# A new order of work for an attention and squared-relu kernel: first states alone, weights ahead of the second input, a sixth batch in seven products

## The chip, the cores and the metric

The kernel runs on one core of a Trainium2 chip. A core has TensorE (PE; its weight loads are shown apart as PEld), VectorE (DVE), ScalarE (ACT), GpSimd (POOL) and SyncE (SP). They work at the same time and wait for each other through semaphores; each runs its own instructions in the order in which the program gives them. Transfers between the chip's memory (HBM) and the on-chip memory (SBUF) are issued on the queues of GpSimd, ScalarE and SyncE and run on 16 shared DMA engines. TensorE writes its results to PSUM, from where the other engines take them. The metric is the device time of one execution in microseconds, as the median of several runs.

## The reference

Eight batches, each with 8 heads, 512 positions, 32 state rows and 64 channels, go through two attentions between x and state; the results become 8 * 544 = 4352 rows of 512 for a two-layer network:

```python
def _attn_ref(x, state):                       # (8,8,512,64), (8,8,32,64)
    scores = scale * np.matmul(x, state.transpose(0, 1, 3, 2))
    a = softmax over the 32 states
    xread = np.matmul(a, state)                # 512 rows per batch
    scores2 = scale * np.matmul(state, x.transpose(0, 1, 3, 2))
    a2 = softmax over the 512 positions
    sread = np.matmul(a2, x)                   # 32 rows per batch
    return np.concatenate([xread, sread], axis=2)

def _moe_ref(x, w_in, w_out, s, b):            # w_in 512x2048, w_out 2048x512
    r = np.maximum(x @ w_in, 0.0)
    g = s * (r * r) + b
    return g @ w_out
```

## The kernel before, in words

All work is cut into pieces. The list `ORDER` (lines 15 to 75) names them in one long sequence, and the last loop of the kernel (lines 724 to 727) calls them in that order. Nothing is moved afterwards: each engine gets its instructions in the order of the words. So `ORDER` alone sets what stands ahead of what on each engine and on each DMA queue. A word is a name and its arguments; a last letter A, V or G names the engine (ScalarE, VectorE, GpSimd) that does the piece.

**Loading.** `x0.g` loads the second half of batch 0's x for the heads of group g; its first half comes in as float32 by SyncE (line 215) and is cast by `castx`. `x.b` loads another batch with two transfers of 256 KB (as float16), `xn.b` the same data in another layout with four. `win.j` loads a quarter of w_in (512 of the 2048 hidden columns, two transfers of 256 KB), `wout.q` a quarter of w_out (512 KB). `st` loads the state rows of all batches but the first two, all on GpSimd's queue. The first two batches' states come on ScalarE's queue (line 216) and are cast by `casts`. `pair` and `turn` bring states into the two layouts that the matmuls want, on VectorE and through TensorE.

**Attention of batch b.** `xT` transposes x (VectorE), `T` makes the scores (TensorE), `keep` copies them out of PSUM (ScalarE), `U` transposes them, `mu` takes the maxima, `D` subtracts, `E1` is the exponential (ScalarE), `z` sums and inverts, `At` multiplies, `A` transposes back: A holds the softmax weights. For batch 0 these run in two halves of the positions (a last argument 0 or 1). `nm`, `nms`, `E2`, `a2`, `aps`, `a2T`, `V` and `srd` are the softmax over positions; all batches' `srd` feed one further small block (`lsr`, `ssr`, `P_sr`, here called the summary rows).

**Layer one.** w_in is first multiplied with a batch's states: `M.b.j` makes four hidden blocks' worth on TensorE, `Mc` casts it out of PSUM. A hidden block is then M times A: `l.b.f` (two matmuls of 512 columns, f from 0 to 15) with a relu on ScalarE; for batch 0, `lh.0.f.p` does blocks f and f+1 for half p. `s` and `sh` square the relus into the tile g on any of the three engines. `ps_h`, the PSUM pool of these blocks, has two buffers.

**Layer two**, plain: `L.b.rr.q` (line 505) adds four of sixteen hidden blocks for 128 rows; `out` evicts with scale and bias (VectorE, line 515) and stores. In seven products (Strassen's scheme in Winograd's form): g and w_out are seen as 2x2 blocks; `wsum.T1` to `T4` make differences of w_out's blocks once, `S` makes sums of g's blocks for a batch, partly in place, `P.b.u` is half of a product (8 matmuls of 256 columns; line 594 through the helper at line 137), `ev` evicts a product (line 604), `put` stores. Batches 3 to 7 and the summary rows use products; 0, 1 and 2 are plain. Both take turns in the two buffers of PSUM pool `ps_o`.

**Fillers.** `idle.n` (line 672) issues n matmuls of 512 columns on ones; nobody reads them.

The parts that the change touches are in `ORDER` and these functions:

Of the kernel before, what the change touches and what calls it, by code (L numbers as in the profile page):

```python
# [15 lines left out]
    "x0.1 x0.0 castx.1.A xT.0.1.0 casts.A idle.12 pair.0.4 castx.0.A xT.0.0.0 T.0.1.0 U.0.0 turn.0.4.A "  # L16
    "mu.0.0 D.0.V.0 E1.0.0 sb idle.12 keep.0.0 xT.0.1.1 win.0 M.1.0.0 M.0.0.1 x.1 z.0.0 xT.0.0.1 At.0.V.0 "
    "A.0.0 win.1 wout.0 T.0.0.1 U.0.1 Mc.1.0.A mu.0.1 D.0.V.1 Mc.0.0.A lh.0.2.0 xT.1.1 lh.0.0.0 keep.0.1 "
    "xT.1.0 idle.5 E1.0.1 win.2 M.0.1.0 T.1.1 sh.0.0.0.V Mc.0.1.A z.0.1 At.0.V.1 A.0.1 lh.0.6.0 lh.0.4.0 "
    "keep.1 sh.0.6.0.V sh.0.4.0.V sh.0.2.0.G L.0.1.0 lh.0.0.1 lh.0.4.1 lh.0.2.1 M.0.2.0 Mc.0.2.A lh.0.6.1 "  # L20
    "L.0.0.0 win.3 l.0.8 l.0.10 M.1.2.1 Mc.1.2.A M.0.3.0 U.1 mu.1 D.1.V l.0.11 sh.0.2.1.V wout.1 l.0.9 "
    "M.1.1.1 wout.2 Mc.0.3.V wout.3 sh.0.0.1.V M.1.3.0 E1.1 l.0.13 l.0.12 st s.0.10.2.V L.0.0.1 L.0.1.1 "
    "z.1 Mc.1.3.A x.2 s.0.12.2.A l.0.15 At.1.V s.0.8.2.G L.0.1.2 l.0.14 A.1 L.0.0.2 l.1.11 l.1.2 cps.0 "
    "s.0.14.2.A cps.1 cps.2 cps.3 Mc.1.1.V l.1.10 s.1.10.2.G l.1.6 L.0.0.3 c bias",
    "l.1.0 l.1.5 pair.4.16 xT.2 sh.0.4.1.V x.3 L.0.1.3 l.1.3 turn.4.12.V out.0.0 out.0.1 l.1.1 T.2.1 U.2 "
    "M.2.3.0 Mc.2.3.A mu.2 D.2.V l.1.9 L.0.3.0 keep.2 l.1.8 l.1.7 xT.3 s.1.8.2.A L.0.2.0 M.2.1.1 "
    "sh.0.6.1.G E1.2 M.2.2.0 l.1.12 Mc.2.1.V z.2 L.0.3.1 L.0.3.2 At.2.V l.1.14 Mc.2.2.A L.0.2.1 L.0.2.2 "
    "s.1.2.2.A s.1.6.2.G l.1.4 s.1.0.2.A A.2 l.1.15 L.0.3.3 out.0.3 l.1.13 x.4 xn.3 T.3.1 M.2.0.0 "
    "s.1.4.2.G l.2.6 U.3 s.1.14.2.V l.2.14 L.1.0.0 Mc.2.0.A l.2.4 nm.3 nms.3.A s.1.12.2.V xT.4 L.1.0.1 "
    "mu.3 D.3.G l.2.13 l.2.5 E2.3.0 L.0.2.3 out.0.2",  # L30
    "l.2.0 E2.3.1 L.1.0.2 L.1.0.3 l.2.7 out.1.0 M.3.0.0 Mc.3.0.A x.5 M.3.1.1 s.2.4.4.V l.2.1 l.2.9 "
    "L.1.1.0 L.1.1.1 E1.3 l.2.3 l.2.8 L.1.1.2 L.1.1.3 M.3.2.0 M.4.0.1 a2.3 Mc.3.1.V z.3 xn.4 At.3.G A.3 "
    "l.2.12 l.2.10 out.1.1 L.1.3.0 Mc.3.2.V l.2.2 L.1.3.1 wsum.T1.2.G s.2.12.2.A l.2.15 s.2.14.2.A l.2.11 "
    "L.1.3.2 Mc.4.0.V L.1.3.3 out.1.3 l.3.6 s.2.0.4.G T.4.1 U.4 l.3.5 l.3.2 aps.3 a2T.3.V l.3.7 L.1.2.0 "
    "nm.4 L.1.2.1 L.1.2.2 L.1.2.3 nms.4.A E2.4.0 xT.5 E2.4.1 l.3.4",
    "l.3.0 M.4.2.1 M.4.1.0 Mc.4.1.A L.2.1.0 Mc.4.2.V L.2.1.1 s.3.4.2.A l.3.11 a2.4 s.3.6.2.A l.3.10 "
    "out.1.2 s.2.8.2.G M.3.3.0 T.5.1 wsum.T3.0.V wsum.T3.1.V nm.5 l.3.1 mu.4 L.2.0.0 L.2.0.1 Mc.3.3.A "
    "nms.5.A E2.5.1 D.4.V E1.4 s.2.10.2.G L.2.1.2 aps.4 l.3.12 U.5 l.3.13 wsum.T2.2.V z.4 x.6 At.4.G "
    "L.2.0.2 L.2.0.3 a2T.4.A l.3.15 l.3.3 turn.12.16.A E2.5.0 L.2.1.3 out.2.1 xT.6 l.3.9 l.3.8 V.3.4 "
    "srd.3 M.5.0.1 l.3.14 out.2.0 Mc.5.0.A L.2.2.0 s.3.0.4.A A.4 L.2.2.1 l.4.1 L.2.3.0 L.2.3.1 l.4.2 "  # L40
    "srd.4 s.3.12.4.V L.2.2.2 L.2.2.3 M.4.3.0 s.3.8.4.V M.5.2.1 nm.2 a2.5 nms.2.V E2.2.0 Mc.4.3.A l.4.3 "
    "Mc.5.2.A out.2.2 L.2.3.2 E2.2.1 L.2.3.3 mu.5 out.2.3 l.4.4",
    "l.4.0 aps.5 P.3.0 a2.2 a2T.5.A S.3.3.2.V s.4.0.2.A s.4.2.2.A xn.5 P.3.1 ev.3.X1 S.3.1.1.V P.3.2 "
    "S.3.1.0.V S.3.2.2.V l.4.7 T.6.1 nm.6 D.5.G E1.5 xn.2 z.5 At.5.G M.5.1.0 P.3.3 l.4.9 Mc.5.1.A P.3.4 "
    "l.4.14 l.4.13 P.3.5 ev.3.Y l.4.5 l.4.6 ev.3.X2 U.6 s.4.4.2.A s.4.6.2.A aps.2 a2T.2.A P.3.6 nms.6.V "
    "wsum.T4.0.V wsum.T4.1.V S.3.4.2.V P.3.7 E2.6.0 P.3.8 l.4.10 l.4.8 ev.3.W1 E2.6.1 V.5.2 srd.2 x.7 "
    "srd.5 P.3.10 s.4.8.2.V P.3.11 xn.6 mu.6 a2.6 l.4.15 l.4.11 A.5 P.3.9 ev.3.X3 S.4.3.0.G aps.6 a2T.6.A "
    "l.4.12 ev.3.W2 l.5.10 s.4.12.4.A P.3.12 P.3.13 M.6.0.0 M.5.3.1 Mc.5.3.A l.5.1 S.4.1.0.V s.4.10.2.V "
    "Mc.6.0.A nm.0 put.3.0.0 P.4.0 l.5.3 P.4.1 l.5.11 ev.3.X4 D.6.V E1.6 P.4.2 S.4.3.1.V S.4.1.1.V P.4.3 "
    "l.5.5 S.4.2.2.V S.4.4.1.G l.5.8 M.6.2.1 ev.4.X1 ev.4.Y z.6 Mc.6.2.A At.6.G M.6.1.0 l.5.2 nms.0.A "  # L50
    "xT.7 l.5.6 E2.0.1 P.4.6 E2.0.0 xn.0 P.4.4 P.4.5 ev.4.X2 A.6 l.5.9 l.5.4 T.7.1 keep.7 P.4.7",
    "l.5.0 S.4.4.0.V l.5.7 s.5.8.4.V P.4.8 P.4.9 nm.7 l.5.13 put.3.0.1 ev.4.W1 Mc.6.1.A l.5.15 P.4.10 "
    "l.5.12 put.3.1.0 ev.4.X3 put.3.1.1 P.4.12",
    "l.6.0 P.4.11 U.7 s.5.4.2.V s.5.6.2.V l.6.11 s.5.0.4.G l.6.2 a2.0 aps.0 nms.7.A mu.7 ev.4.W2 "
    "put.4.0.0 D.7.G xn.7 put.4.0.1 l.5.14 P.4.13 ev.4.X4 P.5.0 a2T.0.A S.5.3.0.V xn.1 l.6.3 V.6.0 srd.0 "
    "M.6.3.1 s.5.14.2.V l.6.8 l.6.10 s.5.12.2.V Mc.6.3.V P.5.1 s.6.2.2.V srd.6 S.5.3.1.V ev.5.X1 l.6.4 "
    "l.6.7 S.5.1.2.V P.5.2 l.6.9 P.5.3 ev.5.Y M.7.1.1 M.7.0.0 l.6.1 S.5.2.2.V Mc.7.0.V P.5.6 Mc.7.1.A "
    "E1.7 l.6.12 P.5.7 ev.5.W1 S.5.4.0.V l.6.6 P.5.4 P.5.5 l.6.14 P.5.10 z.7 S.5.4.1.V M.7.2.0 M.7.3.1 "
    "E2.7.1 l.6.13 l.6.15 ev.5.X2 s.6.6.2.A s.6.12.4.A P.5.8 P.5.9 s.6.0.2.G Mc.7.3.V ev.5.X3 l.6.5 "
    "put.4.1.0 put.4.1.1 s.6.4.2.A P.5.11 ev.5.W2 P.5.12 P.5.13 At.7.G A.7 ev.5.X4 s.6.8.2.G l.7.12 "  # L60
    "put.5.0.0 l.7.14 P.6.0 l.7.4 l.7.15 s.6.10.2.G put.5.0.1 put.5.1.0 S.6.3.2.V P.6.1 S.6.1.2.V E2.7.0 "
    "ev.6.X1 nm.1 Mc.7.2.A l.7.7 a2.7 l.7.13 S.6.2.0.V P.6.2 P.6.3 ev.6.Y l.7.2 l.7.3 aps.7 nms.1.A "
    "E2.1.0 E2.1.1 P.6.4 P.6.6 S.6.4.0.V",
    "l.7.0 l.7.6 S.6.2.1.G P.6.5 l.7.5 a2T.7.V P.6.7 a2.1 aps.1 l.7.8 l.7.10 s.7.12.4.V a2T.1.V S.6.4.1.V "
    "ev.6.W1 V.7.1 srd.1 s.7.6.2.G l.7.1 l.7.11 s.7.0.2.G ev.6.X2 s.7.2.2.G P.6.10 P.6.8 P.6.9 put.5.1.1 "
    "P.6.11 srd.7 ev.6.X3 l.7.9 lsr.3 P.6.12 lsr.1 P.6.13 lsr.2 ssr.2.2.A lsr.8 ev.6.W2 put.6.0.0 "
    "put.6.0.1 s.7.4.2.V P.7.0",
    "lsr.0 lsr.10 P.7.2 lsr.5 ssr.0.2.A s.7.10.2.V ev.6.X4 lsr.6 s.7.8.2.V S.7.3.2.V P.7.1 lsr.11 "
# [10 lines left out]
def kernel(  # L79
# [678 lines left out]
```

## Time and profile before

| | before |
|---|---|
| median of 3 runs (lowest to highest) | 219.09 us (218.51 to 219.42) |
| the profiled execution | 218.68 us |
| its span, first to last instruction | 216.8 us |
| granted TensorE clock, mean | 0.998 |
| PE / DVE / ACT / POOL busy | 207.0 / 169.4 / 154.7 / 105.0 us |
| last matmul of the chain begins | 211.78 us |
| HBM read / written | 25.72 / 8.91 MB |

Busy times are unions over a span that has two quite different stages, the opening with the loads and the rest, so shares of the whole span say little; the views by stretch and the chain of waits say more. In the slices each digit is the busy share of 5.4 us in tenths. A pair of figures such as "602 ns" for a group is the mean of one instruction; matmuls are pipelined, so sixteen in a row take much less than sixteen means, and their pace is read from the chain.

### The profile page before, as it was taken

What the parts mean: (1) busy time and instruction counts of PE and PEld (TensorE: products, weight loads), DVE (VectorE), ACT (ScalarE), POOL (GpSimd) and SP (SyncE); (2) the same over time, 40 slices, a digit from 0 to 9 for tenths busy, and PEclk for the clock granted to TensorE, in tenths of its full rate; (3) what the DMA queues carried; (4) which work ended last, traced back from release to release, by engine and by line L of the source; (5) the groups of instructions that cost most, each with busy time, mean ns of one, the idle gap of its engine ahead of it and who ended that gap; (6) DMA issues with size and microseconds to landing.
All of it is one profiled execution on the core that took longest, in us unless ns stands there. A gap on an engine that the chain in (4) does not pass through costs nothing.

```text
span 216.8 us, 4729 instructions
## 1 busy us (share of the span) xinstructions
PE 207.0 (95%) x1920; PEld 126.4 (58%) x1920; DVE 169.4 (78%) x236; ACT 154.7 (71%) x262; POOL 105.0 (48%) x102
## 2 busy tenths in 40 slices
PE   7668999999999999999999999999999999999992
PEld 2334444344444434545677666776667777888881
DVE  2699885989867879986998799979887964785571
ACT  4378987898858788899889899667668866444400
POOL 8529123494679930525254318836564334225330
PEclk9999999999999999999999999999999999999999
DMA  6999992759497262192908850718903600450055
GB/s 153 186 205 205 199 197 42 125 124 133 106 173 120 48 99 49 38 155 55 144 9 137 139 110 4 97 39 139 205 10 65 131 0 3 87 111 0 0 153 141
DMA packets 23657, 22.42 MB, mean 103 GB/s; under 512 B 4436, under 2 KB 17492, under 8 KB 23636
## 3 DMA queue, kind: packets, MB, share of 16 engines
q0 software_dynamic: 16848, 12.52, 40.8%
q1 hardware_dynamic: 5504, 8.66, 16.4%
q10 hardware_dynamic: 1284, 0.95, 1.6%
q8 instruction: 15, 0.25, 0.5%
q14 instruction: 6, 0.05, 0.1%
HBM read 25.72 MB, written 8.91 MB: 160 GB/s over the span
## 4 chain that ended last, share of the span: by engine, by line
PE 90%; ACT 5%; DMA 2%; DVE 0%; issue 0%; SPq 0%
PE hps L461 24%; PE ops L505 19%; PE opf_X L137 16%; PE opf_W L137 8%; PE mps L137 4%; PE opf_Y L137 4%; PE hps_sr L461 3%; PE vps L137 2%; DMA xf<-in_x_dram 2%; ACT M L152 2%; PE aps L137 2%; PE ops_sr_X L137 2%; PE T_None L137 2%; ACT rh L491 1%; PE dps L672 1%; PE hph L137 1%
## 5 line engine op out<-in xcount | busy, mean ns | idle before, releaser
L465 ACT ACTIVATE r<-hps 128x512 f16<-128x512 f32 x120 | 67.5, 602 | 27.8 <-PE hps L461 26.3
L461 PE MATMUL hps<-A,M 128*128 128x512 f16 x240 | 64.7, 380 | 0.0
L137 PEld LDWEIGHTS <-g 128*128 128x128 f16 x480 | 46.6, 98 | 11.4 <-issue 0.7
L505 PE MATMUL ops<-w_out,g 128*128 128x512 f16 x192 | 46.3, 379 | 0.0
L471 POOL TENSOR_TENSOR g<-r 128x1024 f16<-128x1024 f16 (+1 forms) x14 | 30.4, 2180 | 23.7 <-ACT r L465 23.7
L461 PEld LDWEIGHTS <-M 128*128 128x128 f16 x240 | 21.7, 98 | 22.7 <-issue 6.2
L505 PEld LDWEIGHTS <-g 128*128 128x128 f16 x192 | 18.7, 98 | 22.2 <-issue 0.4
L152 ACT CAST M<-mps 128x1024 f16<-128x1024 f32 x22 | 22.3, 1017 | 1.6 <-PE mps L137 1.5
L469 ACT ACTIVATE g<-r 128x1024 f16<-128x1024 f16 (+1 forms) x18 | 21.4, 1210 | 0.1
L192 POOL DMA_DIRECT2D xn<-in_x_dram x32 | 18.6, 592 | 5.6 <-PE vps L137 4.9
L346 POOL TENSOR_TENSOR At<-E,rz 128x1024 f16<-128x1024 f16 x5 | 9.8, 1964 | 22.0 <-ACT r L465 11.3
L137 PE MATMUL opf_X<-w_T,g 128*128 128x256 f16 x160 | 19.8, 272 | 0.0
L575 DVE TENSOR_TENSOR g<-g 128x1024 f16<-128x1024 f16 (+1 forms) x20 | 17.9, 908 | 1.1 <-POOL S L575 0.9
L575 POOL TENSOR_TENSOR g<-g 128x1024 f16<-128x1024 f16 x4 | 8.8, 2207 | 19.6 <-PE opf_X L137 12.4
L471 DVE TENSOR_TENSOR g<-r 128x1024 f16<-128x1024 f16 (+1 forms) x18 | 14.7, 836 | 1.6 <-ACT r L465 1.6
L152 DVE CAST M<-mps 128x1024 f16<-128x1024 f32 x10 | 12.1, 1213 | 3.5 <-PE mps L137 3.0
L604 DVE SCALAR_TENSOR_TENSOR osx<-opf_X,sb_bc,bias_bc 128x512 f32<-128x512 f32 x15 | 11.2, 746 | 4.0 <-PE opf_X L137 3.9
L292 DVE STREAM_TRANSPOSE xT<-xh 128x1024 f32<-128x1024 f32 (+2 forms) x12 | 10.4, 869 | 4.7 <-ACT xh L152 4.1
L325 POOL TENSOR_TENSOR Dm<-U,mu 128x1024 f32<-128x1024 f32 x3 | 5.7, 1913 | 15.0 <-DVE mu L321 15.0
L465 ACT ACTIVATE r_sr<-hps_sr 128x256 f16<-128x256 f32 x16 | 6.1, 382 | 7.9 <-PE hps_sr L461 7.2
L137 PE MATMUL mps<-w_in,stT 64*32 64x512 f16 x256 | 11.2, 383 | 0.3
L515 DVE SCALAR_TENSOR_TENSOR osb<-ops,sb_bc,bias_bc 128x512 f32<-128x512 f32 x12 | 8.8, 737 | 3.4 <-PE ops L505 3.4
(101 smaller groups left out, 324.3 us busy)
## 6 DMA issues: line engine op xcount, KB each, us to landing
out_dram<-osx SPq DMA_DIRECT2D x36, 128.0 KB, 2.4
xn<-in_x_dram POOLq DMA_DIRECT2D x32, 128.0 KB, 5.1
xh<-in_x_dram POOLq DMA_DIRECT2D x14, 256.0 KB, 5.1
w_in<-in_moe_w_in_dram POOLq DMA_DIRECT2D x8, 256.0 KB, 8.3
w_out<-in_moe_w_out_dram POOLq DMA_DIRECT2D x4, 512.0 KB, 11.2
out_dram<-osb SPq DMA_DIRECT2D x16, 128.0 KB, 2.6
out_dram<-osb SPq DMA_DIRECT2D x16, 64.0 KB, 4.4
xf<-in_x_dram SPq DMA_DIRECT2D x2, 256.0 KB, 3.7
```

The costliest lines, as they stand in the source:

```text
L137: return nc.tensor.matmul(out, lhsT, rhs, start=start, stop=stop, tile_position=tp, is_transpose=is_transpose, skip_group_check=skip,)
L152: (engine.copy if engine is nc.scalar else engine.tensor_copy)(out, in_)
L192: nc.gpsimd.dma_start(out=xn_t[b][32 * jh : 32 * jh + 32].rearrange("t h c d -> t h (c d)"), in_=x[b].rearrange("h (t jh c) d -> jh t h (c ...
L292: nc.vector.transpose(part(out, p, g), part(in_, p, g))
L346: e.tensor_tensor(out, E1, over_n(rz), ALU.mult)
L461: nc.tensor.matmul(hps, lhsT, rhs, start=(i == 0), stop=(i == len(terms) - 1))
L465: nc.scalar.activation(R_t[tag, q][:, i], hps, AF.Relu)
L469: nc.scalar.activation(g, r, AF.Square)
L471: e.tensor_mul(g, r, r)
L505: nc.tensor.matmul(ops_t[tag, rr], G_t[tag][:, f, P * rr : P * rr + P], w_out_f(f), start=(f == 0), stop=(f == NKF - 1),)
L575: e.tensor_tensor(out, x, y, op)
L604: nc.vector.scalar_tensor_tensor(out, fast(b, name[0]), s_bc, out if plus else bias, ALU.mult, ALU.add)
```

## The change

- ScalarE's queue loads only batch 0's states (`stf` has 2 rows of tiles instead of 4); `st` gets a range, and is called twice: `st.2.4` for batch 1 as GpSimd's third transfer, and `st.4.16` for the others. `pair` and `turn` are called three times instead of twice.
- On GpSimd's queue the three first blocks of w_in stand ahead of x.1; `wout.0` follows x.1, then win.3, wout.1, the other states, x.2, wout.2 and wout.3.
- Batch 2's layer two is in seven products: no `L.2` and `out.2`, but `S.2`, `P.2`, `ev.2` and `put.2`, and the `wsum` pieces earlier.
- Fillers: 5 matmuls (2, 2 and 1) instead of 29 (12, 12 and 5).
- The order of everything, and which engine does many of the squares, casts, sums and multiplications, is new. Among them: `castx.0` and `Mc.1.0` on VectorE, `D` of batch 0's second half and `At.1` on GpSimd, and `U.0.1` and `mu.0.1` ahead of `z.0.0`.

The diff, cut to its core (the first group of words in full, then the places of batch 2, and the end):

```diff
-    "x0.1 x0.0 castx.1.A xT.0.1.0 casts.A idle.12 pair.0.4 castx.0.A xT.0.0.0 T.0.1.0 U.0.0 turn.0.4.A "
-    "mu.0.0 D.0.V.0 E1.0.0 sb idle.12 keep.0.0 xT.0.1.1 win.0 M.1.0.0 M.0.0.1 x.1 z.0.0 xT.0.0.1 At.0.V.0 "
-    "A.0.0 win.1 wout.0 T.0.0.1 U.0.1 Mc.1.0.A mu.0.1 D.0.V.1 Mc.0.0.A lh.0.2.0 xT.1.1 lh.0.0.0 keep.0.1 "
-    "xT.1.0 idle.5 E1.0.1 win.2 M.0.1.0 T.1.1 sh.0.0.0.V Mc.0.1.A z.0.1 At.0.V.1 A.0.1 lh.0.6.0 lh.0.4.0 "
-    "keep.1 sh.0.6.0.V sh.0.4.0.V sh.0.2.0.G L.0.1.0 lh.0.0.1 lh.0.4.1 lh.0.2.1 M.0.2.0 Mc.0.2.A lh.0.6.1 "
-    "L.0.0.0 win.3 l.0.8 l.0.10 M.1.2.1 Mc.1.2.A M.0.3.0 U.1 mu.1 D.1.V l.0.11 sh.0.2.1.V wout.1 l.0.9 "
-    "M.1.1.1 wout.2 Mc.0.3.V wout.3 sh.0.0.1.V M.1.3.0 E1.1 l.0.13 l.0.12 st s.0.10.2.V L.0.0.1 L.0.1.1 "
...
+    "castx.1.A xT.0.1.0 castx.0.V xT.0.0.0 casts.A pair.0.2 x0.0 turn.0.2.A xT.0.0.1 x0.1 T.0.1.0 U.0.0 "
+    "st.2.4 keep.0.0 xT.0.1.1 win.0 T.0.0.1 keep.0.1 mu.0.0 pair.2.4 win.1 D.0.V.0 E1.0.0 U.0.1 idle.2 "
+    "idle.2 mu.0.1 win.2 z.0.0 At.0.V.0 turn.2.4.A x.1 D.0.G.1 A.0.0 M.0.0.1 sb Mc.0.0.A idle.1 wout.0 "
+    "E1.0.1 z.0.1 At.0.V.1 A.0.1 M.0.1.0 Mc.0.1.A M.1.0.1 Mc.1.0.V xT.1.0 lh.0.2.0 sh.0.2.0.G lh.0.6.0 "
+    "lh.0.0.0 lh.0.0.1 lh.0.2.1 lh.0.6.1 sh.0.6.0.G xT.1.1 M.0.2.0 win.3 Mc.0.2.A T.1.1 sh.0.0.0.V "
+    "lh.0.4.1 l.0.11 sh.0.0.1.V l.0.9 wout.1 L.0.0.0 U.1 mu.1 D.1.V keep.1 l.0.8 l.0.10 E1.1 M.0.3.0 "
+    "Mc.0.3.V z.1 M.1.1.1 lh.0.4.0 st.4.16 L.0.1.0 Mc.1.1.A l.0.13 sh.0.4.0.V x.2 l.0.14 M.1.2.0 Mc.1.2.V "
+    "pair.4.16 M.1.3.1 l.0.15 L.0.1.1 s.0.8.2.G Mc.1.3.A wout.2 wout.3 l.0.12 turn.4.12.A At.1.G A.1 "
+    "L.0.0.1 s.0.12.2.A s.0.10.2.G l.1.11 s.0.14.2.G xT.2 l.1.2 cps.0 T.2.1 U.2 mu.2 x.3",
+    "l.1.0 l.1.9 L.0.0.2 keep.2 l.1.10 l.1.8 M.2.0.1 D.2.G E1.2 cps.1 Mc.2.0.A cps.2 cps.3 c L.0.0.3 bias "
...
+    "l.2.0 L.1.3.2 s.2.0.2.V M.3.3.0 Mc.3.3.A M.4.2.1 l.2.4 L.1.3.3 l.2.2 L.1.2.0 L.1.2.1 s.2.12.4.A "
+    "L.1.2.2 M.4.1.1 A.3 M.4.0.0 l.3.10 Mc.4.1.A out.1.3 s.2.4.2.G l.3.4 Mc.4.2.V E1.4 wsum.T4.1.V "
+    "wsum.T4.0.V s.2.2.2.V L.1.2.3 out.1.2 l.3.7 P.2.0 P.2.1 l.3.9 wsum.T3.1.V l.3.2 T.5.1 Mc.4.0.A "
+    "wsum.T3.0.V S.2.3.2.V ev.2.X1 l.3.1 P.2.2 l.3.11 l.3.8 s.3.8.4.A nm.5 nms.5.V S.2.1.2.V S.2.2.2.V "
+    "P.2.3 ev.2.Y x.6 z.4 S.2.4.1.G aps.4 l.3.5 E2.5.0 l.3.15 P.2.4 P.2.5 l.3.3 ev.2.X2 P.2.6 xT.6 l.3.14 "
...
-    stf = konst.tile([P, 4, D], FP32, name="stf")
+    stf = konst.tile([P, NG, D], FP32, name="stf")
...
-    nc.scalar.dma_start(stf, rows[:, 0:4])
+    nc.scalar.dma_start(stf, rows[:, 0:NG])
...
-    def load_states():
-        nc.gpsimd.dma_start(stn[:, 4:], rows[:, 4:])
+    def load_states(i0, i1):
+        nc.gpsimd.dma_start(stn[:, i0:i1], rows[:, i0:i1])
...
-        "castx": cast_x, "casts": lambda e: copy(e, stn[:, 0:4], stf), "pair": pair_states, "turn": turn_states,
+        "castx": cast_x, "casts": lambda e: copy(e, stn[:, 0:NG], stf), "pair": pair_states, "turn": turn_states,
```

In the words of the close, before and after, the summary rows' first product and sums change places: before, `P_sr.0` stands ahead of `P.7.10` and `S_sr.2` is two halves on VectorE; after, `P_sr.0` follows `P.7.13`, and `S_sr.2`'s second half is GpSimd's.

## The prediction

> **What bounds the kernel now.** I read the page's busy table and slices first, then the windows by stage, the chain that ended last, the timelines of the opening and of the close, and the landings of the transfers.
>
> ```profile
> PE 207.0 (95%) x1920; PEld 126.4 (58%) x1920; DVE 169.4 (78%) x236; ACT 154.7 (71%) x262; POOL 105.0 (48%) x102
> ...
> PE   7668999999999999999999999999999999999992
> ...
> DMA  6999992759497262192908850718903600450055
> ```
>
> TensorE is full from the fourth slice on; the transfer engines are full in the first six slices (32 us) and half idle later. So there are two stages. Windows, with columns: stretch, its length, busy time and instructions of PE, PEld, DVE, ACT, POOL, then granted clock, DMA share, GB/s:
>
> ```profile
> 20.00:26.00 6.00, 5.55 (x61) 2.33 (x59) 5.35 (x6) 5.41 (x10) 1.58 (x3) 1.00 1.23 200
> 26.00:32.00 6.00, 6.00 (x35) 2.66 (x28) 5.16 (x7) 5.30 (x10) 1.90 (x1) 1.00 1.47 197
> 32.00:213.00 181.00, 180.65 (x1701) 114.38 (x1699) 145.44 (x199) 132.39 (x227) 89.14 (x77) 1.00 0.50 88
> ```
>
> From 26 us on TensorE never waits, so a microsecond of matmuls taken out there is a microsecond off the end, and a faster other engine is worth nothing. Before that, the chain that ended last (start, duration, what) runs over a transfer, filler matmuls and ScalarE's casts:
>
> ```profile
> 1.22 4.38 DMA xf<-in_x_dram
> 8.25 2.70 PE dps L672 x12
> 11.36 1.94 ACT M L152 x2
> ...
> 72.72 3.45 PE ops L505 x16
> ...
> 102.26 1.75 PE opf_X L137 x16
> ```
>
> Timelines of the opening and the close:
>
> ```profile
> 3.14 0.15 PEld L672 LDWEIGHTS <-ones 128*128 128x128 f16 x1 [0.28 <-issue]
> 3.57 0.15 PEld L672 LDWEIGHTS <-ones 128*128 128x128 f16 x1 [0.28 <-issue]
> 3.99 1.02 PEld L672 LDWEIGHTS <-ones 128*128 128x128 f16 x5 [0.28 <-issue]
> ...
> 12.01 0.71 DVE L361 STREAM_TRANSPOSE A<-At 128x512 f16<-128x512 f16 x1
> ...
> 18.24 0.71 DVE L361 STREAM_TRANSPOSE A<-At 128x512 f16<-128x512 f16 x1
> ...
> 212.69 0.48 DVE L706 SCALAR_TENSOR_TENSOR osr<-ops_sr_X,sb_bc,bias_bc 128x256 f32<-128x256 f32 x1 [0.39 <-PE ops_sr_X L137]
> ```
>
> The reader is to see: sixteen plain layer-two matmuls take 3.45 us, sixteen of the product kind 1.75; the first fillers' weight loads are 0.43 us apart, the last five stand within 1.02; the two halves of batch 0's A are there at 12.72 and 18.95; TensorE's last result is evicted from 212.69, and eviction and store take the 4.1 us to the end. The profiled execution took 218.68 us around its 216.8 us span, 0.41 under the 219.09 median. I sum differences and subtract them from the median.
>
> **1. Batch 2 in seven products (gain, on the path).** Gone are four row groups of 16 matmuls at 3.45 us: 13.8. Added are 14 half products of 8 matmuls at 0.875: 12.25. Difference -1.55. Off TensorE, VectorE loses four plain evictions (4 x 0.737 = 2.95) and gets seven product evictions (7 x 0.746 = 5.2) and three full sums (3 x 1.22 = 3.66): +5.9. GpSimd gets two half sums at 2.13. The cover is the idle time of VectorE, 181 - 145 = 36 us in 32 to 213. Stores stay eight of 128 KB on SyncE's queue.
>
> **2. Where that cover is thinnest.** The weight differences T3 and T4, row groups 2 and 3 of batch 1's evictions, and batch 2's sums all come between l.2.0 and P.2.4. Counting from the end of l.2.0 along VectorE's new order with the rows: out.1.3 ends at 3.95 (it waits for L.1.3.3), the M eviction (1.21), two halves of T4 (0.68 each) and a square (0.69) reach 7.2, while TensorE gets to P.2.0 at 8.45. From there out.1.2 (to 8.8), two T3 halves, S.2.3 (1.22), the first eviction (0.75), nm.5 (1.21), a scale (0.14), S.2.1 and S.2.2 (1.22 each) end at 15.9; TensorE reaches P.2.4, which needs S.2.2, after 16.0. So a margin of 0.1 here; at the plain places there is more than 1 us. GpSimd has 20 us more to do in all (words of the order times row means: 102 to 123 us), squares above all, at 1.94 or 3.6 us each. No row shows these neighbours together: from below 0 (the margins hold), from above one late sum per batch, 5 batches x 0.2 = 1.0. I take +0.2, near the lower end, since the same kind of order gave 180.65 busy of 181 us before.
>
> **3. The opening: what lands when.** GpSimd's queue holds eight transfers: the ninth issue (w_out, 6.70) waited for the first landing. It is never empty until 35.5 us. Landings before (issue plus the trace's time to landing): x of batch 0 at 7.3, w_in block 0 at 10.6, x.1 12.85, w_in 1 15.6, w_out quarter 0 17.9, w_in 2 21.2, w_in 3 23.8, w_out quarters 26.5, 29.05, 31.6, states 32.8, x.2 35.5. Bytes are the same after (64 KB less beside them on ScalarE's queue, 32 KB of states inserted), so I keep the spacings (2.55 to 2.8 us a block): w_in 0, 1, 2 at 10.5, 13.1, 15.9, x.1 18.3, w_out 0 20.9, w_in 3 23.7, w_out 1 26.4, states 27.6, x.2 30.3, w_out 2 32.9, w_out 3 35.4. GpSimd's issues stand behind work: w_out.0 behind D.0's second half (it waits for mu.0.1, 11.5, and ends at 12.5), win.3 behind two half squares (1.18 each, done near 18.2), wout.2 and 3 behind s.0.8. All are early enough: w_in 3 needs the queue only at 20.9.
>
> **4. The opening: what computes when.** The cast of x half 0 moves to VectorE (no such row; ScalarE's 0.62 and VectorE's 0.69 for a copy out of PSUM bound it; I take 0.62), and batch 0's state transpose (0.2 by half of 0.27) now stands behind it: T begins near 6.9, not 6.78. VectorE then goes U.0.0 to 8.1, a transpose of x 0.43, mu 0.69, a state transpose 0.2, D 0.69 (10.1), and now U.0.1 0.72 and mu.0.1 0.69 ahead of z.0.0 and its reciprocal 0.93, At 0.65, A 0.71: A.0.0 at 13.8 (was 12.72). The second half needs only z, At and A after that, 2.3: A.0.1 at 16.15 (was 18.95). The half layers run from 14 us, with relus of 0.6 each, to 19.4; T.1 follows x.1 to 20.2; four l of batch 0 and L.0.0.0 to 23.2; M.0.3 waits for w_in 3 until 23.8. By 23.85 the old kernel had done one half layer (0.44) and one quarter group of L (0.86) more, and two l (0.86) fewer: the new one is 0.45 behind. Then T.2 waits for x.2 and its transpose (30.3 + 1.2 = 31.5) at a point TensorE reaches at about 31.2: 0.3. Filler matmuls, 29 before and 5 after, only fill waits now; the 2.70 us ones on the old chain are paid for by M.0.0 waiting for w_in 0 to land at 10.5 in either kernel. Sum of the opening +0.7; bounds -0.5 (blocks land 0.6 sooner, no wait for x.2) and +1.8 (each late by 0.5 more).
>
> **5. The close.** The last summary layer, its sums and products keep their shapes; S_sr.2 goes half to GpSimd (1.1 us) and is done about 3.2 us after the last summary hidden block starts, P_sr.2 reached at 3.9. Cost 0, tail 4.1 as before.
>
> **Sum:** -1.55 + 0.2 + 0.7 = -0.65; 219.09 - 0.65 = 218.4.
>
> **A rule against the change.** The first seven filler matmuls are 0.43 us apart, the last five about 0.22, though the granted clock reads 1.00 throughout. So this trace shows TensorE at half pace in its first 2.7 us of work, and the new order opens with no filler: its first dense stretch is the half layers at 14 us. At half pace those take 0.87 each instead of 0.44 and, until 18 us, are hidden by the wait for w_in 3: sum unmoved. The Trainium skill, "TensorE: Matmul & The Clock Gate", Part 1, says that half rate is the default, that about 3.4 us of sustained work releases it and an idle window as long brings it back; the trace agrees on the release, and no run shown has the return. By that rule the gaps after each transfer could bring it back, and the sum would be that of the second rival.
>
> **Rivals.**
> *The opening is even or ahead.* For it: the second half of A is 2.8 us sooner and M.0.1 and M.0.2 have their weights 2.5 and 5.3 us sooner. Against: w_in 3, x.2 and w_out end where they ended. With -0.5 for the opening: -1.55 - 0.5 + 0.1 = about -2.0, 217.1.
> *TensorE stays at half pace (ends slower).* The work from 14.2 to 23.8 us is about 6.5 us at full pace. At half pace throughout it takes 13, to 27.2: +3.4, that is 221.8. The wait for w_in 3 hides it up to about 19.5; after that each us at half pace costs 0.5. The gain is gone at about 21 us, and the kernel is slower by over 1.1 us if half pace lasts past 23. For it: 24 fewer filler matmuls and gaps from 7 to 14 us. Against: the old kernel, with PE busy 1.58 of 3 us at 11 to 14, kept its pace.
> *VectorE or GpSimd becomes the bound near the sums.* With margins of 0.1 and sums on GpSimd of 2.13, a delay of 0.2 to 0.4 in each of six product batches gives back 1.2 to 2.4: 219.1 to 220.7, 219.9 in the middle. Against: VectorE's 36 us of idle.
>
> **Numbers.** About 0.5%, 1.1 us, is what a measurement of this kernel tells from no change. Forecast 0.38 (0.12 of it faster by more, 0.26 within). Opening ahead 0.30, all faster. Half pace 0.14 (0.11 slower, 0.03 within). VectorE or GpSimd 0.18 (0.11 slower, 0.07 within). Together faster 0.42, same 0.36, slower 0.22. The range runs from 216.3 (opening ahead by 1.3) to 220.8 (the upper end of the VectorE case), leaving the long half pace out. The forecast's own range is 217.4 to 219.4.
>
> **What would show it.** Step 1: 64 matmuls fewer at L505, 112 more of the product kind, none waiting. Step 2: PE 99% busy between 36 us and the end; if not, a wait on S or on a VectorE eviction near P.2.4 names the rival. Step 3: w_in 3 landing near 23.7, x.2 near 30. Step 4: A's two transposes ending near 13.8 and 16.2, M.0.3 near 23.8; and the spacing of the first half layers' weight loads tells half pace (0.22 for 256 columns) from full (0.11). I am wrong if the transfers' order moves landings by more than a microsecond, since nearly all the opening hangs on them.

## The result

| | before | after |
|---|---|---|
| median of 20 runs (lowest to highest) | 219.01 us (218.26 to 220.32) | 220.62 us (219.03 to 221.40) |
| the profiled execution | 218.68 us | 220.73 us |
| its span | 216.8 us | 219.0 us |
| the last product of the summary rows begins | 211.78 us | 213.97 us |

The ratio is 1.0071, with a 95% interval of 1.0053 to 1.0089: the changed kernel is 0.7% slower, by 1.6 us. I had forecast 0.65 us faster. The time lies inside my range; the direction was wrong.

The lines of functions stand one further down in the new kernel: layer one's matmuls are L462, layer two's plain ones L506, the product helper L138, the eviction of a product L605, the sums S L576, stores L614, w_in's loads L201. First its page, with the busy table and the slices:

```profile
PE 204.5 (93%) x1944; PEld 129.2 (59%) x1944; DVE 174.0 (79%) x238; ACT 153.1 (70%) x257; POOL 127.6 (58%) x114
...
PE   0799889999999999999899999999999999999992
...
DMA  6999999359980390006707390698663600170046
```

TensorE works 2.5 us less than before and the span is 2.2 us longer, so it waits more than it did. The saving is small for what was taken out: the fillers alone went from 8.1 to 2.5 us and the products save 1.55, so the other matmuls take some 4.7 us longer; the opening runs at half pace for longer (below). One slice in the middle (the twentieth, 104 to 110 us) shows an 8 where before there were only nines. The windows say where; columns are the stretch, its length, busy time and instructions of PE, PEld, DVE, ACT, POOL, then granted clock, DMA share and GB/s:

```profile
20.00:26.00 6.00, 4.80 (x38) 1.98 (x36) 4.49 (x4) 4.77 (x9) 4.39 (x6) 1.00 1.10 156
26.00:32.00 6.00, 6.00 (x48) 2.43 (x46) 4.89 (x8) 5.73 (x9) 5.12 (x5) 1.00 1.44 197
32.00:213.00 181.00, 179.27 (x1736) 118.11 (x1733) 149.07 (x198) 131.34 (x223) 105.27 (x84) 1.00 0.49 86
100.00:120.00 20.00, 18.89 (x202) 13.28 (x201) 18.36 (x28) 15.36 (x28) 13.42 (x13) 1.00 0.60 103
120.00:213.00 93.00, 93.00 (x991) 70.79 (x989) 73.21 (x102) 62.69 (x110) 48.62 (x36) 1.00 0.45 80
```

From 20 to 26 us TensorE is busy 4.80 us (5.55 before) and the transfers move 156 GB/s (200 before). From 100 to 120 it misses 1.11 us. From 120 on it is full. What TensorE waited for, in us in total, times, longest:

```profile
PE sps L138 <- DMA ident<-ident_const: 5.2, 1, 5.2
PE mps L138 <- DMA w_in<-in_moe_w_in_dram: 1.4, 2, 1.0
...
PE opf_W L138 <- DVE osx L605: 0.7, 1, 0.7
...
PE T_None L138 <- DVE xT L293: 0.6, 1, 0.6
PE opf_X L138 <- POOL g L576: 0.4, 1, 0.4
```

The first is the start: without the old fillers TensorE's first matmul comes at 5.25 us, where the old kernel's came at 1.46. The second and fourth belong to the opening (M.0.1 and M.0.3, and T.2), the third and fifth to the middle, and all are waits of the new order. The chain that ended last (start, duration, what) ties the opening's together:

```profile
5.07 8.12 DMA w_in<-in_moe_w_in_dram
13.23 1.05 PE mps L138 x12
14.28 0.98 PE hph L138 x4
15.28 0.61 ACT rh L492
15.97 2.03 POOL g L472 x2
18.00 1.24 POOL w_in L201 x2
19.24 0.77 POOL w_out L207
20.01 1.03 POOL stn L230
21.04 0.50 POOL xh L184
21.54 9.93 DMA xh<-in_x_dram
31.56 1.26 DVE xT L293
32.86 0.64 PE T_None L138 x16
...
213.97 0.89 PE ops_sr_X L138 x8
```

Read it from the top: w_in's second block lands at 13.19, M.0.1, the first half layers, their relu, two half squares on GpSimd, and only then the two issues of w_in's fourth block, with everything that follows on that queue, down to x.2, which T.2 waits for. The trace has w_in's fourth block issued at 17.95 and 18.62, and the quarter of w_out ahead of it had fully landed at 21.14. The transfers move 198 and 207 GB/s in the two microseconds from 17 to 19 us, then 151 to 172 from 19 to 23, 100 from 23 to 24, and 205 again from 25 to 26: the queue ran thin behind the late issue. The block landed at 23.23 and 24.64.

In the middle, VectorE's timeline has the first eviction of batch 3's products with 1.32 us of idle ahead of it:

```profile
106.09 0.75 DVE L605 SCALAR_TENSOR_TENSOR osx<-opf_X,sb_bc,bias_bc 128x512 f32<-128x512 f32 x1 [1.32 <-PE hps L462]
106.75 1.21 DVE L337 TENSOR_REDUCE z<-E 128x32 f32<-128x1024 f16 x1
108.00 0.35 DVE L338 RECIPROCAL rz<-z 128x32 f32<-128x32 f32 x1
108.27 0.65 DVE L605 SCALAR_TENSOR_TENSOR osx<-opf_Y,sb_bc,osx 128x512 f32<-128x512 f32 x1
```

The matmul that is named as its releaser (PE hps) is not one that it reads, so it was another. The evicted tile `osx0` exists once (`bufs=1`), and batch 2, now in products too, had just written it. Its four stores were issued from 98.57 to 100.44; the last of them landed at 105.91, 5.5 us after its issue and 0.18 us ahead of the eviction. The transfers issued from 97 to 108 us (KB each, median us from issue to landing):

```profile
out_dram<-osx SPq DMA_DIRECT2D x8, 128.0 KB, 4.6
xn<-in_x_dram POOLq DMA_DIRECT2D x4, 128.0 KB, 5.7
```

Over the whole run such a store takes 2.7 us; here four loads of `xn` were issued from 99.61 on, beside them. That the loads slowed the stores is likely but not shown: no run moves them away. The late eviction puts the second one (opf_Y) at 108.27, after which TensorE may take the bank again (0.7 us of wait), and puts VectorE's and GpSimd's sums late (0.4 us more).

### The profile page after: what moved, and what is told of

Its sections match the earlier page's. It is cut to its first block, busy times and chain, and to the rows that moved or that the text cites. A ratio compares the mean times of both kernels' runs of the same rounds, so it can differ in the third digit from the quotient of the medians.

```text
span 219.0 us, 4791 instructions
## 1 busy us (share of the span) xinstructions
PE 204.5 (93%) x1944; PEld 129.2 (59%) x1944; DVE 174.0 (79%) x238; ACT 153.1 (70%) x257; POOL 127.6 (58%) x114
## 4 chain that ended last, share of the span: by engine, by line
PE 81%; DMA 8%; POOL 5%; DVE 3%; issue 1%; ACT 0%; POOLq 0%; DVEq 0%
PE hps L462 22%; PE opf_X L138 19%; PE ops L506 11%; PE opf_W L138 9%; PE opf_Y L138 5%; DMA xh<-in_x_dram 5%; DMA w_in<-in_moe_w_in_dram 4%; PE mps L138 4%; PE hps_sr L462 3%; PE vps L138 2%; PE aps L138 2%; PE ops_sr_X L138 2%; POOL w_in L201 1%; PE T_None L138 1%; POOL g L576 1%; POOL g L472 1%
## 5 line engine op out<-in xcount | busy, mean ns | idle before, releaser
L462 PE MATMUL hps<-A,M 128*128 128x512 f16 x240 | 65.2, 380 | 0.2 <-ACT rh L492 0.2
L138 PEld LDWEIGHTS <-g 128*128 128x128 f16 x576 | 56.0, 98 | 15.1 <-issue 1.2
L472 POOL TENSOR_TENSOR g<-r 128x1024 f16<-128x1024 f16 (+1 forms) x10 | 27.5, 2749 | 24.2 <-ACT r L466 24.2
L462 PEld LDWEIGHTS <-M 128*128 128x128 f16 x240 | 21.6, 98 | 21.6 <-issue 6.6
L506 PE MATMUL ops<-w_out,g 128*128 128x512 f16 x128 | 31.6, 379 | 0.0
L576 POOL TENSOR_TENSOR g<-g 128x1024 f16<-128x1024 f16 x10 | 21.2, 2122 | 17.6 <-PE hps L462 10.8
L153 ACT CAST M<-mps 128x1024 f16<-128x1024 f32 x23 | 23.7, 1045 | 2.5 <-PE mps L138 2.5
L138 PE MATMUL opf_X<-w_T,g 128*128 128x256 f16 x192 | 24.1, 273 | 0.4 <-POOL g L576 0.4
L506 PEld LDWEIGHTS <-g 128*128 128x128 f16 x128 | 12.2, 98 | 14.8 <-issue 0.8
L472 DVE TENSOR_TENSOR g<-r 128x1024 f16<-128x1024 f16 (+1 forms) x19 | 17.6, 943 | 3.9 <-ACT r L466 3.9
L605 DVE SCALAR_TENSOR_TENSOR osx<-opf_X,sb_bc,bias_bc 128x512 f32<-128x512 f32 x18 | 13.4, 742 | 9.2 <-PE opf_X L138 4.3
L576 DVE TENSOR_TENSOR g<-g 128x1024 f16<-128x1024 f16 (+1 forms) x20 | 18.9, 955 | 0.3
L347 POOL TENSOR_TENSOR At<-E,rz 128x1024 f16<-128x1024 f16 x6 | 11.5, 1913 | 12.6 <-DVE rz L338 11.6
L470 ACT ACTIVATE g<-r 128x1024 f16<-128x1024 f16 (+1 forms) x13 | 18.7, 1453 | 0.1
L138 PE MATMUL mps<-w_in,stT 64*32 64x512 f16 x256 | 12.7, 404 | 1.4 <-DMA w_in<-in_moe_w_in_dram 1.4
L138 PE MATMUL opf_W<-w_T,g 128*128 128x256 f16 x96 | 12.1, 272 | 0.7 <-DVE osx L605 0.7
L326 POOL TENSOR_TENSOR Dm<-U,mu 128x1024 f32<-128x1024 f32 (+1 forms) x4 | 7.6, 1903 | 8.1 <-DVE mu L322 8.1
L138 PE MATMUL opf_Y<-w_out,g 128*128 128x256 f16 x96 | 12.3, 273 | 0.0
```

Of the source, the lines that this page charges most:

```text
L138: return nc.tensor.matmul(out, lhsT, rhs, start=start, stop=stop, tile_position=tp, is_transpose=is_transpose, skip_group_check=skip,)
L153: (engine.copy if engine is nc.scalar else engine.tensor_copy)(out, in_)
L347: e.tensor_tensor(out, E1, over_n(rz), ALU.mult)
L462: nc.tensor.matmul(hps, lhsT, rhs, start=(i == 0), stop=(i == len(terms) - 1))
L470: nc.scalar.activation(g, r, AF.Square)
L472: e.tensor_mul(g, r, r)
```

## The experiments

The ratios are against runs of the kernel before on the same chip, whose medians were 218.84 to 219.09 us. Differences between kernels are given below with each kernel's own median of before subtracted first: the changed kernel is 1.61 us above it, the kernels with the fourth block earlier, with two tiles and with both are 0.71 above, 0.45 above and 0.49 below. "Last product" is the begin of the summary rows' last product in the profiled execution, 211.78 before and 213.97 after; from 120 us on TensorE is full in both, so it says when all before it was done.

| kernel | median us | ratio (95% interval) | last product |
|---|---|---|---|
| fourth block of w_in issued earlier | 219.55 | 1.0032 (1.0015 to 1.0048) | 212.44 |
| two evicted tiles | 219.29 | 1.0016 (0.9997 to 1.0035) | 211.58 |
| both | 218.36 | 0.9977 (0.9955 to 0.9999) | 211.22 |
| both, fillers first | 218.49 | 0.9986 (0.9965 to 1.0006) | 212.08 |
| both, fillers that hold the clock | 218.72 | 0.9997 (0.9979 to 1.0016) | 211.83 |
| fillers first alone | 220.61 | 1.0079 (1.0057 to 1.0101) | 213.70 |
| two tiles, x.1 ahead of w_in 1 | 221.38 | 1.0106 (1.0085 to 1.0126) | 214.38 |
| batch 2 plain | 222.89 | 1.0174 (1.0141 to 1.0207) | 213.79 |
| batch 2 plain, w_in 3 earlier | 221.62 | 1.0129 (1.0109 to 1.0149) | 213.60 |
| old first group of words | 225.14 | 1.0281 (1.0258 to 1.0303) | 217.93 |
| old first two groups | 224.88 | 1.0268 (1.0251 to 1.0285) | 218.35 |
| old order, products put in | 231.81 | 1.0599 (1.0572 to 1.0626) | 224.21 |

### The fourth block of w_in issued ahead of the squares

```diff
-... lh.0.2.0 sh.0.2.0.G lh.0.6.0 ... M.0.2.0 win.3 Mc.0.2.A ...
+... lh.0.2.0 win.3 sh.0.2.0.G lh.0.6.0 ... M.0.2.0 Mc.0.2.A ...
```

> The changed kernel with one word moved: the issue of w_in's fourth block stands ahead of GpSimd's two half squares of batch 0. Theory (the late issue emptied the queue, so every later landing slid by about 1.2 us): the block lands by 23.8 instead of 24.64 us, w_out and x.2 a microsecond sooner too, M.0.3 begins near 23.8, the time drops by 1.0 to 219.6 us. Rival (the transfer engines were slow for another reason, or TensorE's half pace carries the opening): landings and time move by less than 0.3 us, 220.4 or more.

Measured 219.55, which is 0.90 us less than the changed kernel. The fourth block was issued at 13.06 instead of 17.95. The block itself landed at 24.50, hardly sooner than 24.64 and not by 23.8 as expected; but w_out's second quarter, x.2 and w_out's last quarter landed at 26.77, 30.49 and 35.60 (27.75, 31.47 and 36.60 in the changed kernel): all about 1 us sooner. So the late issue is one of the causes, for about a microsecond. The timed runs carry this more than the landings, since two executions with the late issue had landings as early as these; the section on TensorE's pace says why.

### Two buffers for the evicted tile of the first row half

```diff
-... tag=f"osx{key}", bufs=1)
+... tag=f"osx{key}", bufs=2 if key == "0" else 1)
```

> The changed kernel with a second buffer for the tile in which products are evicted for the first two row groups, so that batch 3's first eviction need not wait for batch 2's stores to land. Theory: VectorE's 1.3 us wait at 106.1 us goes, and with it TensorE's waits of 0.72 at 108.3 and 0.39 at 112.2; time 1.1 lower, 219.5 us. Rival (VectorE and GpSimd are simply too full there): the waits move by less than 0.2 and the time stays at 220.4 or more.

Measured 219.29, which is 1.16 us less than the changed kernel. The eviction now starts at 103.71, and TensorE has no gap in the same window:

```profile
103.71 0.74 DVE L598 SCALAR_TENSOR_TENSOR osx<-opf_X,sb_bc,bias_bc 128x512 f32<-128x512 f32 x1
```
```profile
100.00:120.00 20.00, 20.00 (x261) 14.66 (x260) 19.68 (x30) 17.14 (x30) 13.39 (x12) 1.00 0.58 94
```

The stores themselves were no quicker (5.5 us at the median); nobody waits for them. The relus of layer one run 0.97 us later in the changed kernel than here up to 104 us and 2.38 later from 117 us on, so the wait for the stores, with what followed it, cost 1.41 us in the profiled execution. It is the second buffer that shows that the eviction waited for the stores; the trace alone does not name them.

### Both together

> The changed kernel with both edits that helped alone: w_in's fourth block issued ahead of the half squares, and two buffers for the evicted first row groups. Theory (the late issue costs 0.8, the wait for stores 1.2, and they lie in different places): 220.4 - 2.0 = 218.4 us, a ratio of 0.998. Rival (the two are one delay seen twice, since the first run showed a shorter store wait too): 219.2.

Measured 218.36: 0.94 less than with two buffers alone and 1.20 less than with the earlier issue alone. So the two costs add up, and without them the change is a gain of 0.2% (0.01% to 0.45%). It has the lowest median of the study. The windows from 20 us of the changed kernel, and then of this one, show the hole in the transfers closed (last column, GB/s):

```profile
20.00:23.00 3.00, 2.82 (x16) 1.15 (x13) 2.93 (x3) 2.63 (x5) 2.13 (x4) 1.00 1.16 160
23.00:26.00 3.00, 1.98 (x24) 0.83 (x23) 1.56 (x2) 2.14 (x5) 2.25 (x2) 1.00 1.04 151
```
```profile
20.00:23.00 3.00, 2.92 (x16) 1.15 (x13) 2.93 (x3) 2.89 (x5) 0.99 (x2) 1.00 1.24 206
23.00:26.00 3.00, 2.62 (x27) 1.12 (x26) 2.19 (x3) 2.78 (x6) 2.26 (x2) 1.00 1.56 191
```

### x.1 ahead of w_in's second block

```diff
-... pair.2.4 win.1 D.0.V.0 ... turn.2.4.A x.1 D.0.G.1 ...
+... pair.2.4 x.1 win.1 D.0.V.0 ... turn.2.4.A D.0.G.1 ...
```

> The changed kernel with two buffers for the evicted row groups (219.3 us so far) and x.1 put back on the queue ahead of w_in's second block, as in the old load order. Theory (the new sequence of matmuls wants w_in's second block at 13 us, and x.1 not before 18): the block lands near 15.8, the half layers of the second block and all behind them start up to 2.5 us later, part of it absorbed by the later wait for w_in's fourth block: 220.3 to 221.3 us. Rival (batch 1's attention is what the opening waits for): 218.8 or less.

Measured 221.38, 2.08 more than the two-buffer kernel that it is made from. w_in's second block landed at 15.65 instead of 13.21, the half layers and with them GpSimd's half squares came later, and the fourth block behind those was issued only at 20.42. The queue then ran nearly dry (41 GB/s from 20 to 23 us, 152 from 23 to 26). So the new place of w_in's blocks is right for this order; a good part of the 2.08 is the same late issue, made worse, and the run does not separate the two.

### The pace of TensorE: fillers first, and fillers that hold the clock

```diff
-"castx.1.A xT.0.1.0 castx.0.V ...
+"idle.12 castx.1.A xT.0.1.0 castx.0.V ...
```

> The changed kernel with the old twelve filler matmuls put first again; nothing else. The clock records of the runs so far show full pace from 4.1 us in the old kernel but only from 11.5 to 17.2 us in the executions of the new opening. Theory (the late release of the clock is a part of the opening's loss, about 0.5 us of it, and of its spread): full pace from about 4 us, the first half layers 0.44 instead of 0.87 us, the end 0.3 to 0.8 sooner, 219.6 to 220.1 us, with less spread. Rival (the opening waits for transfers, and half pace is hidden behind them): no change, 220.4, with the weights landing where they did.

Measured 220.61: nothing gained. The windows of this run show why it says little on the price:

```profile
5.00:12.00 7.00, 4.42 (x54) 1.65 (x51) 6.64 (x15) 2.41 (x7) 4.58 (x8) 1.00 1.17 164
12.00:19.00 7.00, 6.21 (x37) 3.01 (x37) 5.10 (x9) 4.92 (x8) 2.79 (x4) 0.52 1.17 195
19.00:40.00 21.00, 19.83 (x174) 8.06 (x173) 15.99 (x19) 18.13 (x28) 17.62 (x18) 1.00 1.15 173
```

The granted clock was back at half from 11.94 to 18.76 us, in an opening with gaps. The same fillers on top of both mends:

> Both mends and the twelve fillers first. Theory (clock release worth 0.5 on its own): 217.9 us, faster than the kernel before by 0.4%. Rival (fillers hidden or in the way): as the run with both mends alone, 218.4.

Measured 218.49 beside 218.36: no gain, and again full pace only from 7.01 to 10.43 and then from 17.25. So I put fillers into the gaps as well (12 first, 8 after the first scores, 5, 5 and 5 where the new order had 2, 2 and 1, which is 6 and 4 more around the casts, and 3 more behind M.0.1):

> The kernel with both mends (win.3 ahead of the half square, two buffers for the evicted tile of row group 0) and filler matmuls placed so that TensorE has no long gap from about 4 us on (12 first, 8 after the first scores, 9 and 1 more around the casts, 3 after M.0.1). It prices the half pace of TensorE. Theory that half pace costs something: granted full pace from about 5 us on and not given back, the bias copy 0.3 to 1.0 us sooner than with the mends alone (37.24), time 217.6 to 218.0. Rival, that half pace lies wholly beside the waits for w_in: the same pace, the bias copy unmoved, 218.2 to 218.6.

Now full pace was granted from 4.31 us to the close, and the time was 218.72. The bias copy, a mark that all of these kernels have after the same work, came at 37.85 against 37.24 with both mends and no fillers. So with the issue moved up, half pace in the opening had no price that these runs could show; that the fillers themselves took time is possible, and a loss of a few tenths under them can't be excluded.

With the late issue it is another matter. Five profiles have the fourth block of w_in behind the half squares; in all of them the issue hangs on the same chain, which begins when w_in's second block lands (us from the start):

| kernel | full pace for good from | second block landed | fourth block issued | in between | x.2 landed | bias copy |
|---|---|---|---|---|---|---|
| batch 2 plain | 11.53 | 12.84 | 16.93 | 4.09 | 30.41 | 37.51 |
| two evicted tiles | 12.17 | 13.21 | 17.31 | 4.10 | 30.50 | 37.60 |
| the changed kernel | 15.82 | 13.19 | 17.95 | 4.76 | 31.47 | 38.57 |
| fillers first alone | 18.76 | 13.71 | 18.47 | 4.76 | 31.54 | 38.64 |
| two tiles, x.1 ahead of w_in 1 | 20.85 | 15.65 | 20.42 | 4.77 | 33.29 | 40.40 |

Where full pace came before the block had landed, the chain took 4.1 us; where it came later, 4.8. Its first matmuls, M.0.1, show the pace, first in the changed kernel, then with two tiles:

```profile
13.23 1.05 PE L138 MATMUL mps<-w_in,stT 64*32 64x512 f16 x15 [0.33 <-DMA w_in<-in_moe_w_in_dram]
```
```profile
13.26 0.62 PE L131 MATMUL mps<-w_in,stT 64*32 64x512 f16 x15 [0.63 <-DMA w_in<-in_moe_w_in_dram]
```

So half pace made the issue 0.7 us later, and x.2 landed 1 us later in the changed kernel than with two tiles. The first three rows have the same words up to the bias copy. With the issue moved up the bias copy follows no such order: full pace from 16.35, 17.24 and 18.39 us went with 37.24, 37.74 and 37.53 (both mends; the issue alone; the issue with batch 2 plain). No run holds full pace with the late issue in place, so how much of its price is the half pace's was not timed.

### Batch 2 plain in the new order

The words `P.2`, `S.2`, `ev.2` and `put.2` give way to `L.2` and `out.2` at the same places; T3 and T4 stay.

> The changed kernel with batch 2's layer two plain again: the 14 half products replaced in place by 16 quarter groups, sums and product evictions left away, four plain evictions put in. Theory: 13.8 instead of 12.25 us of matmuls (+1.55), but batch 3 has no stores to wait for (-1.1): +0.45, 221.1 us, with no wait of TensorE for evictions near the first products. Rival (the products cost elsewhere all that they save, even without the store wait): 219.5 or less; rival (VectorE bound later anyway): 222 or more.

Measured 222.89, against 219.29 for the two-buffer kernel, which has the same opening and no wait for stores either. The profiled executions differ by 2.21 at the last product. Timed it is 3.6; both profiled executions were the fastest of their runs, 1.7 and 0.9 us under the medians, so the profiles show less of it. I did it once more on the mended opening (`win.3` moved as in the first experiment):

> The kernel with both mends (218.36), but batch 2's layer two plain in the changed kernel's order (T3 and T4 stay where the products want them, one buffer for the evicted tile, which no store of batch 2 holds now). The products' worth with the mended opening, timed a second way after the earlier pair (222.89 against 219.29 timed, 2.1 apart in the profiles). Theory: the products bring 1.6 to 2.1, so 219.9 to 220.5, and TensorE's last matmul 1.6 to 2.2 after the one with both mends (212.1), at 213.7 to 214.3. Rival (the earlier pair's timed 3.6 is real and its profile was a lucky execution): 221.9 or more.

Measured 221.62, 3.0 more than with both mends, and 2.38 at the last product. In this order the products are worth at least the 1.55 us that I had summed. The rest is not all explained: the plain pieces stand where the products' did, not where they would be best, and the time from the last product to the end of the span was 5.6 us in both of these kernels and 5.0 to 5.1 in all others, the kernel before included. Their last store took 2.9 and 2.8 us to land, where it took 2.3 in the changed kernel and with two tiles; why is open.

### The old opening and the old order

> The old kernel's opening, word for word up to the bias, then the new order for everything that is left (batch 2 in seven products). Theory (the opening costs 2.4 us, products give 1.55, the store wait takes 1.1): 219.0 - 1.55 + 1.1 = 218.6 us, and TensorE at 99% after 40 us but for the store wait. Rival (the new order loses its time in the middle): 220 us or more.

With the old kernel's first group of words ahead of the new rest the time was 225.14. The two orders do not fit: in 34 to 37.8 us TensorE is busy 1.79 of 3.8 us, since T.2 and its transposes now come behind the bias row. This says nothing on the new opening. So I tried the seam later, after two groups:

> The first two lines of the order before (its whole opening up to the second line's end) and then the changed kernel's order, with two buffers for the evicted tile of row group 0: the products without the new opening, with a better seam than in the earlier try. Theory (the new opening costs 1.4 to 2.4 us, the products bring 1.55, the store wait cost 1.2): 218.84 - 1.55 = 217.3, and no PE wait over 0.5 us from 40 us on. Rival (the opening is not what costs, or the products bring less): 218.8 or more with TensorE full behind the seam.

Measured 224.88. TensorE is full from 80 us on (and 20.00 of 20 in 100 to 120), but from 40 to 80 it misses 5.1 us. The chain runs there over GpSimd (D, a multiplication, two differences of w_out, squares), and after the longest wait the clock falls. Windows, and then TensorE's timeline:

```profile
70.00:74.00 4.00, 1.18 (x6) 0.42 (x5) 0.75 (x1) 1.26 (x4) 3.92 (x5) 1.00 0.31 66
74.00:77.40 3.40, 3.40 (x9) 1.20 (x8) 1.97 (x5) 2.96 (x7) 0.00 (x0) 0.50 0.98 154
77.40:80.00 2.60, 2.60 (x26) 0.94 (x25) 2.60 (x5) 1.22 (x2) 0.00 (x0) 1.00 0.00 0
```
```profile
73.36 0.59 PE L455 MATMUL hps<-A,M 128*128 128x512 f16 x2 [2.82 <-ACT r L459]
73.79 1.69 PE L499 MATMUL ops<-w_out,g 128*128 128x512 f16 x4
...
78.28 1.04 PE L499 MATMUL ops<-w_out,g 128*128 128x512 f16 x4
```

Four matmuls of 512 columns take 1.69 us at half pace and 1.04 behind it, and in the trace their starts are 0.43 apart instead of 0.21.

> The order before with nothing changed but batch 2's layer two in seven products, its pieces put where the plain ones stood and T3 and T4 made earlier, and two buffers for the evicted tile of row group 0. It isolates the products. Theory: 1.55 us of matmuls less on a full TensorE, 217.3, PE busy 205.4. Rival (VectorE or GpSimd late around batch 2's sums, since nothing else was rearranged for them): 218.5 or more, with TensorE waiting for a sum S or an eviction near 95 to 112 us.

The third try left the old order as it was and put only batch 2's products in (with T4 made earlier, two evicted tiles, and the first states in the memory of one of the products' sums, as in the try before). Measured 231.81, the worst of all. TensorE is busy but for 1.2 us from 40 to 86 us and then waits for batch 2's sums, which VectorE reaches late:

```profile
PE opf_X L130 <- DVE g L568: 6.3, 1, 6.3
PE hps L454 <- ACT r L458: 4.1, 3, 2.8
```
```profile
86.35 1.24 DVE L310 STREAM_TRANSPOSE U<-T_None 128x1024 f32<-128x1024 f32 x1
87.51 1.18 DVE L538 TENSOR_TENSOR w_T<-w_out,w_T 128x2048 f16<-128x2048 f16 x1
88.61 1.21 DVE L329 TENSOR_REDUCE z<-E 128x32 f32<-128x1024 f16 x1
89.86 0.35 DVE L330 RECIPROCAL rz<-z 128x32 f32<-128x32 f32 x1
90.13 4.00 DVE L568 TENSOR_TENSOR g<-g 128x2048 f16<-128x2048 f16 x2
```

The differences of w_out, a transpose and two sums stand in one row on VectorE, and TensorE waits 6.3 us for the last; here too the clock falls to half behind the wait, from 90.42 to 97.25 us. So a clean measurement of the products under the old opening or in the old order failed three times, each on a new wait that the mixing of the orders made; it stays open. What the runs do show is that the products only pay with the rest rearranged around them.

## Why the prediction was wrong

**Step 1, the products: the matmuls right, the stores put at nothing.** 64 plain matmuls fewer, 112 of the product kind more and 24 fillers fewer make 1944 instead of 1920. The two pairs with batch 2 plain show the gain, in this order, to be at least the 1.55 us of the sum. The sentence "Stores stay eight of 128 KB on SyncE's queue" was true and missed the point: plain layer two evicts into `osb`, the products into the one `osx0`, and with a sixth batch in products batch 3's first eviction has to wait until batch 2's stores have landed. I counted the stores and did not ask whose buffer they hold. That cost 1.2 us (timed, with two buffers instead of one), the larger of the two costs that the sum lacked.

**Step 2, the thin margins: not seen, and the rival's price came from elsewhere.** TensorE did not wait near P.2.4. The waits on an eviction and on a sum came with batch 3, both behind the stores; with two buffers TensorE is busy 20.00 of 20 us there. So my +0.2 was 0, and the rival "VectorE or GpSimd becomes the bound near the sums", whose band of 219.1 to 220.7 holds the measured 220.62, came near the price by luck and was wrong in mechanism. (The band does not follow from its own 1.2 to 2.4 us either: with -1.55 and +0.7 these give 219.4 to 220.6.) In the old order (the last experiment) that mechanism does decide.

**Step 3, the transfers: the step that failed.** I had the issue right: w_in's fourth block stands behind two half squares, "done near 18.2" (18.00 in the chain). "All are early enough: w_in 3 needs the queue only at 20.9" was wrong: an issue just ahead of that moment is too late. Issued at 16.93 and 17.31 in two other executions, 4.0 and 3.6 us ahead of it, the block left the later landings near my 26.4, 30.3 (x.2) and 35.4 (at most 26.74, 30.50 and 35.64); issued at 17.95, 2.95 us ahead, they came at 27.75, 31.47 and 36.60, and the block itself at 24.64 where I had 23.7. I had also taken the landing as fixed, whatever TensorE's pace; but the issue hangs on the half layers, and these ran at half pace. At full pace the half squares would have been done by 17.4, so that my 18.2 for them was met only because of the half pace. With the issue moved up the time falls by 0.9 us, with one buffer or two.

**Step 4, what computes when: right in the front part, late behind.** A's halves ended at 13.10 and 15.93 (I said 13.8 and 16.15; the cast on VectorE took 0.43, not 0.62). M.0.3 went on with its last operands at 24.68 (23.8), T.2 began at 32.86 (31.5). I gave the opening +0.7. In the profiled execution it cost 2.3: 213.97 - 211.78 = 2.19 in all, plus the 1.55 that the products bring, less the 1.41 behind the stores. (The same words took 1 us less in two other executions, with full pace sooner: the bias copy at 37.51 and 37.60, not 38.57.) With both mends the same count gives 211.22 - 211.78 + 1.55 = 1.0, and what this last microsecond consists of was not taken apart.

**Step 5, the close: right.** From the last product to the end of the span it is 5.0 us in both kernels.

The sum, by medians: -1.55 for the products, +1.16 for the stores, +0.90 for the late issue, and +1.10 left for the rest of the opening and the margins make the measured +1.61. I had +0.9 for that rest. So without the two costs that I missed the sum about stands, and the kernel with both mends, 0.5 us faster than before where I had forecast 0.65, is close to the kernel that I thought I was predicting. Part of that closeness may be luck: where the products bring more than 1.55, the opening costs as much more.

**The rivals.** "The opening is even or ahead" is out: even mended it is about 1 us behind. "TensorE stays at half pace" got its mechanism right: the new opening is granted full pace only at 11.5 to 17.2 us in most executions, and the pace can come back to half. It did not act as I had priced it. I let the wait for w_in 3 hide the half pace up to about 19.5; in the changed kernel the half pace helped to make that wait longer, by putting the issue 0.7 us later. With the issue moved up its price was nil, since full pace from 4.31 us on gained nothing. I had written that no run showed the return; now six do: one after a wait of 2.82 us that ended at 73.36 (the old first two groups), one at 37.83 (the old first group), one at 90.42 (the old order), and three in openings with gaps. The Trainium skill, "TensorE: Matmul & The Clock Gate", Part 1, says that the pace is decided by activity over free-running windows of 3413 ns, so that the same kernel can differ from run to run; stretches of 3.41 and 6.83 us in these runs, and a release at 11.53, 12.17 and 15.82 us with the same words up to there, agree.

## What to carry to other kernels

When an issue stands behind work on its engine, it has to come well ahead of the time at which the queue would be empty: here 3.6 us ahead was enough and 2.95 was not. Follow the work that it stands behind as far back as it goes, here to TensorE's pace. When a path is used by one more tile of work in a row, look at each buffer of that path and at who frees it last, stores included; a store with loads issued beside it took twice its usual time here (5.5 us instead of 2.7). A gain that is only a sum of matmul times is worth what the neighbours on the other engines leave of it: the same 1.55 us were a loss of 12.9 us in the old order, where little else was moved.

## What the runs showed of the hardware

- Stores of 128 KB landed 2.7 us after their issue over the whole run, and 4.6 us (5.5 in another kernel) with four loads of 128 KB beside them.
- On GpSimd's queue, w_in's fourth block issued at 16.93 or 17.31 us left the later loads in step (x.2 at 30.41 and 30.50); issued at 17.95 or 18.47, all later loads landed about 1 us later (x.2 at 31.47 and 31.54).
- From the landing of w_in's second block to that issue, over matmuls, casts, a relu and two half squares, it was 4.1 us in two executions at full pace and 4.8 in three at half.
- Half pace came back in the middle of a run, not only in the opening, after TensorE had waited 2.82 us in one kernel and 6.3 in another; in the first, matmuls of 512 columns then started 0.43 us apart instead of 0.21 for 3.41 us, which is 1.7 us lost.
- The same opening ended up to 1.1 us apart in different executions (bias copy at 37.51 to 38.57 us with the same words up to there), so one profile of an opening full of transfers is not enough to price it.
